# Tail tiles of two attention units searched as one group, and the last keys of a group transposed together

## Chip, cores and metric

The kernel runs on one core of a Trainium2 chip. The metric is the device time of one execution in microseconds; the median of three runs of the kernel before is 1433.77 us (1432.75 to 1434.97). One execution was recorded by the hardware profiler; its span is 1435.2 us. Engines are named as in the profile: PE (TensorE; PEld is its weight load), DVE (VectorE), ACT (ScalarE), POOL (GpSimd), SP (the queue that issues most transfers).

## The reference

A top-k attention is followed by a mixture of experts without dropping. Everything is float32.

```python
# attention: batch 8, heads 8, sequence 576, head width 64
scores = scale * np.matmul(q, k.transpose(0, 1, 3, 2))
kth = np.partition(scores, -32, axis=-1)[..., -32:-31]
scores = np.where(scores >= kth, scores, -1e9)
attn = softmax(scores)                    # exp, sum + 1e-9
attn_out = np.matmul(attn, v)
# experts: 4608 tokens of width 512, 8 experts, hidden width 1024
x = attn_out laid out as (8 * 576, 512)
logits = x @ w_gate
expert_idx = argmax(logits); gate_w = softmax(logits)[expert_idx]
y = relu(x @ w1[expert_idx]) @ w2[expert_idx]   # per token
return gate_w[:, None] * y
```

For each of the 8 x 8 x 576 query rows the 32nd largest of 576 scores has to be found; that is the search which the change regroups.

## The kernel before

**Units and tiles.** Two heads make a unit (128 partitions: two heads of width 64), so there are 4 units a batch and 32 in all. A head has 576 query rows, that is four tiles of 128 rows and a rest of 64. In a unit, tiles 0 to 3 are the first head's full tiles, 4 to 7 the second head's, and tile 8 (the tail) holds the 64 last rows of both heads, in the two halves of the partitions. `groups` (L215) lists what is searched together: four pairs (i, 4+i), and the tail alone, as a group of one tile. That gives 5 groups a unit, 20 a batch, 160 in all (`work`, L721).

**One group.** `products` (L240) multiplies queries with keys on PE into PSUM, in two halves of 288 keys. `scores` (L256) copies them to SBUF on ACT. `fold` and `fold_on` (L263, L273) take, on DVE, the maximum and the minimum of pairs of scores, so that few candidates remain (168 columns a tile). `search` (L296) finds the 32nd largest with MAX8 (L309, L322) and MATCH_REPLACE8 (L329), four rounds. `depths` (ACT, L352), `less` (POOL, L361) and `weights` (ACT exponential, L372) turn the scores into unnormalised weights with zeros for what isn't selected. `transposed` (L377) turns the weights on PE: four transposes of 128 keys a tile (L385) and one of the last 64 keys a tile (L394), each copied out by ACT (L388 or L390 to `wT`, L397 to `wTt`).

**The end of a unit.** `outputs` (L399) multiplies the transposed weights with the values (L413), in two halves of 288 query rows. Each head has its own 64 output rows in PSUM, and for each head there are four products with `wT` (128 keys each) and one with `wTt`, whose upper 64 partitions are zeros. Then the result is transposed back and multiplied with the gate weights (L419 to L424). `divisors` (DVE, L434), `logits` and `rows` (POOL, L443, L453) apply the softmax sums. `ending` (L783) is a generator that puts these steps at named places of the following groups.

**Order.** `loop` (L879) goes over the groups, and the order of the instructions on PE, ACT and DVE is the order in which the code is written. In group i, DVE first folds group i+1 (L896), then searches group i; the second part of the fold (`fold_on`) is put ahead of the last round of that search. PE is three groups ahead with score products (`AHEAD`, L709), and transposes the group before.

**Expert work as filler.** When a batch's rows are routed, they are scattered to buckets, and full blocks of 128 rows are put through an expert on PE. A block is 16 pieces. `pieces` (L752) puts some of them between the attention's operations; a credit that grows with the group's tiles, times a share that depends on the group's place in the unit (L909 to L918), says how many. The first pieces come in the third batch; what can't be ready earlier is done after the attention, on PE with little else.

In the code below, the lines to follow are the tail's special cases (`len(tiles)`), the last-key transposes, and the products with `wTt`.

Of the kernel before, what the change touches and what calls it, by code (L numbers as in the profile page):

```python
# [35 lines left out]
def kernel(  # L36
# [39 lines left out]

    nc = tc.nc
    B, U, P, _, S = qk.shape
    N, Dm = out.shape
    E = moe_w_gate.shape[1]  # L80
# [33 lines left out]
    def open_pools(st, exact):  # L114
        for name, bufs in (
            ("load", 2), ("att", 2), ("wtp", 1), ("xp", 1 if exact else 2), ("small", 2),
            ("wp", 1 if exact else 2), ("mlp", 2),
        ):
            setattr(k, name, st.enter_context(tc.tile_pool(name=name, bufs=bufs)))
        for name, bufs in (("ps_s", 2), ("ps_t", 2), ("ps_m", 2)):  # L120
            pool = tc.tile_pool(name=name, bufs=bufs, space=bass.MemoryType.PSUM)
            setattr(k, name, st.enter_context(pool))
        k.exact = exact
        k.apart = False
        k.unit = 0

    def load_unit(b, u, parts=False):
        n = SimpleNamespace(b=b, u=u)
        qkb = k.load.tile([P, 2, S], F32, name="qkb")
        if parts:  # L130
            nc.scalar.dma_start(qkb[:, 0, 0:P], qk[b, u, :, 0, 0:P])
            nc.sync.dma_start(qkb[:, 1, :], qk[b, u, :, 1, :])
            nc.scalar.dma_start(qkb[:, 0, P:S], qk[b, u, :, 0, P:S])
        else:
            nc.sync.dma_start(qkb, qk[b, u, :, :, :])
        n.q, n.k = qkb[:, 0, :], qkb[:, 1, :]
        return n
# [43 lines left out]
    for n in range(2):  # L181
        t = const.tile([P, KC * P], F32, name=f"oT{n}")
        nc.gpsimd.memset(t[:, S:], 0.0)
# [4 lines left out]
    wTt = const.tile([P, 2, S], F32, name="wTt")  # L188
    nc.gpsimd.memset(wTt[ST:P, :, :], 0.0)
# [25 lines left out]
    groups = [(i, NC + i) for i in range(NC)] + [(2 * NC,)]  # L215
# [13 lines left out]
    def open_unit(n):  # L229
        n.z = k.small.tile([P, NT], F32, name="z")  # L230
        n.over = None if k.exact else doubt[:, n.b * U + n.u, :, :]
# [8 lines left out]
    def products(n, tiles):  # L240
        todo = []
        got = []
        for i in tiles:
            ps = k.ps_s.tile([P, 2, SM], F32, name="sc")
            todo += [(ps, h, rows, cols) for h, rows, cols in parts(i)]
            got.append(ps)
        for half in range(2):
            for ps, h, rows, cols in todo:
                j = half ^ h if len(tiles) == 1 else half
                d = slice(h * D, (h + 1) * D)  # L250
                nc.tensor.matmul(  # L251
                    ps[rows, j, 0:HF], n.q[d, cols], n.k[d, j * HF:(j + 1) * HF], start=True, stop=True
                )
# [9 lines left out]
    def fold(tiles, s):  # L263

        m2 = slice(0, len(tiles))
        f = SimpleNamespace()
        f.h = k.att.tile([P, 2, HF], F32, name="h", bufs=1)
        nc.vector.tensor_tensor(f.h[:, m2, :], s[:, m2, 0, :], s[:, m2, 1, :], op=ALU.max)  # L268
        f.l = k.att.tile([P, 2, HF], F32, name="l")
        nc.vector.tensor_tensor(f.l[:, m2, :], s[:, m2, 0, :], s[:, m2, 1, :], op=ALU.min)  # L270
        return f

    def fold_on(tiles, f):  # L273

        m2 = slice(0, len(tiles))
        f.few = k.att.tile([P, 2, LW], F32, name="few", bufs=3)
        nc.vector.tensor_tensor(f.few[:, m2, 0:QF], f.h[:, m2, 0:QF], f.h[:, m2, QF:HF], op=ALU.max)
        f.hl = k.att.tile([P, 2, QF], F32, name="hl", bufs=1)
        nc.vector.tensor_tensor(f.hl[:, m2, :], f.h[:, m2, 0:QF], f.h[:, m2, QF:HF], op=ALU.min)
# [16 lines left out]
    def search(n, tiles, s, f, then=lambda: None):  # L296

        m_all = range(len(tiles))
        m2 = slice(0, len(tiles))
# [14 lines left out]
        def quiet(r):  # L314

            return r >= (1 if len(tiles) == 2 else 2)

        for r in range(R):
            if r == R - 1:
                then()  # L320
            for m in m_all:
                nc.vector.max(out=tops[:, m, r * 8:(r + 1) * 8], in_=src[m])  # L322
                if quiet(r):
                    tick()
            if r == 0:
                in_turn(nc.gpsimd.tensor_scalar_mul(nbias[:, m2], tops[:, m2, 0], -scale))
            if r < R - 1:
                for m in m_all:
# [4 lines left out]
                    if quiet(r):  # L333
# [4 lines left out]
        nc.scalar.activation(low[:, m2], thr[:, m2], AF.Copy, scale=STEEP)  # L338

        def doubts():  # L340
            c = 2 * tiles[0] if len(tiles) == 2 else 2 * NC
            k.last_pool = in_turn(nc.gpsimd.tensor_tensor(
                n.over[:, c:c + len(tiles), :], f.few[:, m2, QF + 7:LW:8], _inner(thr[:, m2], NL), op=ALU.subtract
# [4 lines left out]
    def depths(tiles, s, low):  # L348

        w = k.att.tile([P, 2, S], F32, name="w", bufs=1 if k.exact else 3)  # L350
        for m in range(len(tiles)):
# [6 lines left out]
    def less(tiles, s, w):  # L358

        for m in range(len(tiles)):  # L360
# [4 lines left out]
    def weights(n, tiles, w, nbias, beside=()):  # L365

        c = 2 * tiles[0] if len(tiles) == 2 else 2 * NC
        for m in range(max(len(tiles), len(beside))):
            for step in beside[m:m + 1]:
                step()  # L370
            if m < len(tiles):
                nc.scalar.activation(  # L372
                    w[:, m, :], w[:, m, :], AF.Exp, scale=scale, bias=nbias[:, m:m + 1],
                    accum_out=n.z[:, c + m:c + m + 1],
                )

    def transposed(n, tiles, w):  # L377

        pair = len(tiles) == 2
        if tiles[0] == 0:  # L380
            n.wT = k.wtp.tile([P, NC, 2, S], F32, name="wT")
        for m, i in enumerate(tiles):
            pm = bank("wTm")
            for c in range(NC):
                nc.tensor.transpose(pm[:, c * P:(c + 1) * P], w[:, m, c * P:(c + 1) * P], ident)  # L385
            pm4 = pm[:, :].rearrange("p (c q) -> p c q", c=NC)
            if pair:
                nc.scalar.copy(n.wT[:, :, m, tiles[0] * P:(tiles[0] + 1) * P], pm4)  # L388
            else:
                nc.scalar.copy(n.wT[:, :, :, SM:S], pm4.rearrange("p c (h q) -> p c h q", h=2))  # L390
        yield
        pt = bank("wTl")
        for m in range(len(tiles)):
            nc.tensor.transpose(pt[0:ST, m * P:(m + 1) * P], w[:, m, SM:S], ident)  # L394
        yield
        q = slice(tiles[0] * P, (tiles[0] + 1) * P) if pair else slice(SM, S)
        nc.scalar.copy(wTt[0:ST, :, q], pt[0:ST, 0:len(tiles) * P].rearrange("p (h q) -> p h q", h=2))  # L397

    def outputs(n, x):  # L399

        oT = oT_of[k.unit % 2]
        k.unit += 1
        for j in range(2):
            q = slice(j * HF, (j + 1) * HF)
            po = bank("po")
            for c in range(KC):
                for h in range(2):
                    r = slice(h * D, (h + 1) * D)
                    if c < NC:
                        lhsT, rhs = n.v[:, c, r], n.wT[:, c, h, q]  # L410
                    else:
                        lhsT, rhs = n.v[:, c, r], wTt[:, h, q]
                    nc.tensor.matmul(po[r, 0:HF], lhsT, rhs, start=(c == 0), stop=(c == KC - 1))  # L413
            yield
            nc.scalar.copy(oT[:, q], po[:, 0:HF])  # L415
            yield
        px = bank("px")
        for t in range(NC):
            nc.tensor.transpose(px[:, t * P:(t + 1) * P], oT[:, t * P:(t + 1) * P], ident)  # L419
        pl = bank("pl")  # L420
        nc.tensor.transpose(pl[:, 0:P], oT[:, SM:], ident)
        lw = 2 * E
        for t in range(KC):
            nc.tensor.matmul(  # L424
                pl[:, P + t * lw:P + (t + 1) * lw], oT[:, t * P:(t + 1) * P],
# [288 lines left out]
    with fast:  # L714
# [6 lines left out]
        work = [(b, u, g) for b in range(B) for u in range(U) for g in groups]  # L721
        per_batch = U * len(groups)
# [60 lines left out]
        def ending(b, u):  # L783
# [11 lines left out]
            yield "relu"  # L795
            next(out_steps)
            yield "small"
            div = divisors(n)
            aside.append(div)
            yield "products"  # L800
# [67 lines left out]

        def turning(i):
            b, u, g = work[i]  # L870
            return transposed(unit[b * U + u], g, w_of.pop(i))

        def multiply(i):
            b, u, g = work[i]
            got_of[i] = products(unit[b * U + u], g)
            if g == groups[-1] and b * U + u + 2 < len(units):
                unit.append(load_unit(*units[b * U + u + 2]))

        def loop():  # L879
# [7 lines left out]
            f_of[0] = fold(work[0][2], s_of[0])  # L887
            fold_on(work[0][2], f_of[0])
            for i, (b, u, g) in enumerate(work):
                n = unit[b * U + u]  # L890
                if g == groups[0]:
                    open_unit(n)

                then = lambda: None
                if i + 1 < len(work):
                    f_of[i + 1] = fold(work[i + 1][2], s_of[i + 1])  # L896
                    then = lambda: fold_on(work[i + 1][2], f_of[i + 1])
                low, nbias, doubts = search(n, g, s_of[i], f_of.pop(i), then)
                at_place("small")
                w_of[i] = depths(g, s_of[i], low)  # L900
                less(g, s_of.pop(i), w_of[i])
# [11 lines left out]
                if b == B - 1 and at >= ARRIVED:  # L913
                    room -= KEEP
                    credit = room * len(g) / sum(len(x[2]) for x in work[i:])
                share = 0.5 if g in (groups[0], groups[-2]) else 1.6 if g == groups[2] else 1.2 if g == groups[1] else 1
# [15 lines left out]
                weights(n, g, w_of[i], nbias)  # L932
# [4 lines left out]
                if g == groups[-2]:  # L937
# [10 lines left out]
            for count, _ in enumerate(late[0][0]):  # L948
                if count == 4:
                    pieces(4)  # L950
            kept = left - ALWAYS * PIECES
            assert kept == KEEP - 4, kept
# [21 lines left out]
    with ExitStack() as outer:  # L974
# [10 lines left out]
        with ExitStack() as st:  # L985
# [7 lines left out]
            with tc.For_i(0, B, 1) as b:  # L993
# [3 lines left out]
                for u in range(U):  # L997
                    n = load_unit(b, u)
                    load_values(n)
                    open_unit(n)  # L1000
                    for g in groups:
                        s, steps = scores(products(n, g))
                        for step in steps:
                            step()
                        low, nbias, _ = search(n, g, s, None)
# [75 lines left out]
```

## Time and profile before

| Engine | busy us | share of the span | instructions |
|---|---|---|---|
| PE | 1288.2 | 90% | 8034 |
| PEld | 874.8 | 61% | 8034 |
| DVE | 1132.7 | 79% | 4717 |
| ACT | 937.0 | 65% | 2097 |
| POOL | 645.4 | 45% | 838 |

| Operation | count in the trace | mean ns |
|---|---|---|
| fold, L268, 128x576 / 128x288 | 128 / 32 | 827 / 437 |
| fold, L277, 128x288 / 128x144 | 128 / 32 | 544 / 877 |
| MAX8 of 168 columns, L322 | 1152 | 321 |
| transpose of 128 keys, L385 | 1152 | 295 |
| transpose of the last 64 keys, L394 | 288 | 297 |
| product with `wT`, L413 | 1024 | 447 |
| product with `wTt`, L413 | 256 | 406 |
| copy to `wTt`, L397, 64x256 / 64x128 | 128 / 32 | 361 / 245 |

A share of busy time is a mean over the span. The attention ends at about 1163 us, and DVE has nearly nothing to do after that, so its 79% of the span is nearly all of the attention's time. A product of float32 leaves two records in the trace, a transpose leaves one. Records of PE overlap, so a mean duration is longer than the step from one start to the next, and it is the step that counts when PE is full. Shapes of L277 show an oddity that matters later: the smaller form has the longer mean.

### The profile page before, as it was taken

The numbers are of one execution on the slowest core, as the hardware profiler recorded it, in microseconds if no ns is written. First come the engines' busy times: TensorE is split into PE (matmuls) and PEld (weight loads), VectorE is DVE, ScalarE is ACT, GpSimd is POOL, SyncE is SP. The second block draws the span as 40 slices with busy tenths as digits, with TensorE's granted clock in tenths as the row PEclk, the third lists the DMA queues.
The fourth block names the chain that finished last, engine by engine and source line by source line (L and its number), as shares of the span: only waits on it lengthen the run. The fifth ranks groups of instructions, "written<-read, shape, count | busy, mean of one in ns | idle before, by whom it ended". The sixth has DMA issues, their size and how long they took to land. (4 is left out here: it accounts for less than half of the span.)

```text
span 1435.2 us, 25500 instructions
## 1 busy us (share of the span) xinstructions
PE 1288.2 (90%) x8034; PEld 874.8 (61%) x8034; DVE 1132.7 (79%) x4717; ACT 937.0 (65%) x2097; POOL 645.4 (45%) x838
## 2 busy tenths in 40 slices
PE   5777787767799989998999999999999999999995
PEld 3444454444566656665766666666667677777673
DVE  7999999999999999999899999999989950000000
ACT  5777777777787778877777778787777751111110
POOL 3445455445555655565454555565446541000000
PEclk8777788897899999999999999999999999999998
DMA  2000011001664166416553464237541749998880
GB/s 76 27 26 26 26 34 52 27 26 47 234 219 151 54 246 217 150 49 244 216 212 112 161 247 158 100 125 283 201 180 51 264 161 327 391 321 318 324 320 22
DMA packets 102224, 230.69 MB, mean 161 GB/s; under 512 B 5182, under 2 KB 25918, under 8 KB 102080
## 3 DMA queue, kind: packets, MB, share of 16 engines
q1 hardware_dynamic: 95328, 208.71, 41.1%
q0 software_dynamic: 6464, 19.97, 3.8%
q8 instruction: 65, 1.06, 0.3%
q14 instruction: 79, 0.65, 0.1%
q10 hardware_dynamic: 288, 0.30, 0.1%
HBM read 207.68 MB, written 22.33 MB: 160 GB/s over the span
## 5 line engine op out<-in xcount | busy, mean ns | idle before, releaser
L361 POOL TENSOR_TENSOR w<-s,w 128x576 f32<-128x576 f32 x288 | 407.6, 1433 | 512.4 <-ACT w L352 512.4
L667 PE MATMUL ph<-xTs,w 128*128 128x128 f32 x2560 | 320.6, 279 | 3.4 <-ACT xTs L644 3.4
L667 PEld LDWEIGHTS ph<-xTs,w 128*128 128x128 f32 x2560 | 302.3, 193 | 34.3 <-issue 29.3
L682 PE MATMUL py<-w,hT 128*128 128x512 f32 x640 | 295.1, 598 | 1.0 <-ACT hT L672 0.7
L322 DVE MAX8 tops<-scr 128x8 f32<-128x168 f32 x864 | 252.5, 321 | 2.3
L251 PE MATMUL sc<-qkb 64*128 64x288 f32 (+1 forms) x1280 | 231.5, 484 | 24.2 <-ACT s L260 19.9
L372 ACT ACTIVATE w<-w,nbias 128x576 f32<-128x576 f32 x288 | 224.6, 789 | 1.5 <-POOL w L361 1.4
L385 PE MATMUL wTm<-ident,w 128*128 128x128 f32 x1152 | 177.7, 295 | 46.5 <-ACT oT L415 25.9
L352 ACT ACTIVATE w<-s,low 128x576 f32<-128x576 f32 x288 | 209.4, 769 | 5.3
L385 PEld LDWEIGHTS wTm<-ident,w 128*128 128x128 f32 x1152 | 138.5, 150 | 100.4 <-ACT oT L415 34.1
L969 DVE CAST any_i<-pd 1x1 int32<-1x1 f32 x1 | 0.1, 147 | 236.7 <-PE pd L967 236.7
L682 PEld LDWEIGHTS py<-w,hT 128*128 128x128 f32 x640 | 113.5, 190 | 111.0 <-issue 107.0
L251 PEld LDWEIGHTS sc<-qkb 64*128 64x128 f32 (+1 forms) x1280 | 120.0, 201 | 99.8 <-issue 41.1
L329 DVE MATCH_REPLACE8 scr<-tops,scr 128x168 f32<-128x168 f32 x576 | 178.6, 314 | 0.0
L260 ACT COPY s<-sc 128x576 f32<-128x576 f32 x288 | 171.3, 644 | 7.2 <-PE sc L251 7.2
L388 ACT COPY wT<-wTm 128x512 f32<-128x512 f32 x256 | 139.5, 601 | 32.4 <-PE wTm L385 32.1
L413 PE MATMUL po<-wT,vb 128*64 128x288 f32 x1024 | 153.6, 447 | 0.6 <-ACT wT L390 0.6
L688 POOL DMA_INDIRECT out_dram<-y,xg x40 | 43.5, 1087 | 212.7 <-ACT y L696 200.5
L268 DVE TENSOR_TENSOR h<-s 128x576 f32<-128x576 f32 (+1 forms) x160 | 119.9, 749 | 18.2 <-ACT s L260 18.2
L309 DVE MAX8 few<-l 128x8 f32<-128x288 f32 x288 | 128.2, 445 | 0.0
L413 PEld LDWEIGHTS po<-wT,vb 128*64 128x64 f32 x1024 | 73.6, 148 | 76.3 <-issue 24.1
L672 ACT ACTIVATE hT<-ph 128x512 f32<-128x512 f32 x80 | 47.8, 598 | 107.1 <-PE ph L667 105.7
(125 smaller groups left out, 1549.6 us busy)
## 6 DMA issues: line engine op xcount, KB each, us to landing
w<-in_moe_w_dram SPq DMA_DIRECT2D x80, 2048.0 KB, 9.2
qkb<-in_qk_dram SPq DMA_DIRECT2D x31, 576.0 KB, 3.8
xg<-x_rows SPq DMA_DIRECT2D x40, 257.0 KB, 9.8
vb<-in_v_dram SPq DMA_DIRECT2D x32, 320.0 KB, 3.1
x_rows<-blank SPq DMA_DIRECT2D x5, 257.0 KB, 10.1
x_rows<-blank POOLq DMA_DIRECT2D x4, 257.0 KB, 8.6
x_rows<-x,posi POOLq DMA_INDIRECT x40, 3.1
out_dram<-y,xg POOLq DMA_INDIRECT x40, 5.9
```

Of the source, the lines that this page charges most:

```text
L251: nc.tensor.matmul(ps[rows, j, 0:HF], n.q[d, cols], n.k[d, j * HF:(j + 1) * HF], start=True, stop=True)
L260: lambda m=m, ps=ps: nc.scalar.copy(s[:, m, :, :], ps[:, :, 0:HF]) for m, ps in enumerate(got)
L322: nc.vector.max(out=tops[:, m, r * 8:(r + 1) * 8], in_=src[m])
L329: nc.vector.match_replace(out=scr[:, m, :], in_to_replace=tops[:, m, r * 8:(r + 1) * 8], in_values=src[m], imm_value=NEG,)
L352: nc.scalar.activation(w[:, m, :], s[:, m, :, :].rearrange("p j k -> p (j k)"), AF.Relu, scale=-STEEP, bias=low[:, m:m + 1],)
L361: k.last_pool = in_turn(nc.gpsimd.tensor_tensor(w[:, m, :], s[:, m, :, :].rearrange("p j k -> p (j k)"), w[:, m, :], op=ALU.subtract)).ins
L372: nc.scalar.activation(w[:, m, :], w[:, m, :], AF.Exp, scale=scale, bias=nbias[:, m:m + 1], accum_out=n.z[:, c + m:c + m + 1],)
L385: nc.tensor.transpose(pm[:, c * P:(c + 1) * P], w[:, m, c * P:(c + 1) * P], ident)
L388: nc.scalar.copy(n.wT[:, :, m, tiles[0] * P:(tiles[0] + 1) * P], pm4)
L413: nc.tensor.matmul(po[r, 0:HF], lhsT, rhs, start=(c == 0), stop=(c == KC - 1))
L667: nc.tensor.matmul(ph[:, f, :], n.w1[:, 0, dt, fc * P:(fc + 1) * P], n.xT[:, dt, :], start=(dt == 0), stop=(dt == DT - 1),)
L682: nc.tensor.matmul(py, hT[:, f, :], n.w2[:, 0, f, :], start=(f == 0), stop=(f == FT - 1))
```

## The change

Two edits go together.

First, the tails of two neighbouring units (u, u+1) form one group of two tiles, placed between the four pairs of u and the four pairs of u+1. There are 9 groups for two units, 18 a batch and 144 in all, and every group has two tiles. The branches for a group of one tile go.

Second, the last 64 keys of a pair's two tiles are transposed together. For this the keys are laid out on the host with the last 64 also in front of them: the first head's tile is multiplied with the keys in their usual order and has its last 64 keys at its end; the second head's tile takes the order that begins with the last 64 keys. The end of one tile's weights and the start of the next are then 128 neighbouring columns, which one transpose turns into 128 partitions: one head's last keys in the upper half, the other's in the lower half. The values get a last block of the same form, with zeros where a head's keys meet the other head's columns, so that one product of full width replaces the two of 64 rows. `wT` and `wTt` become fixed tiles with room for the tails of an even unit behind, and of an odd unit ahead of, the other query rows.

```diff
-    groups = [(i, NC + i) for i in range(NC)] + [(2 * NC,)]
+    def groups(u):
+        first, second = ([((a, i), (a, NC + i)) for i in range(NC)] for a in (u, u + 1))
+        return first + [((u, 2 * NC), (u + 1, 2 * NC))] + second
...
-        nc.vector.tensor_tensor(f.h[:, m2, :], s[:, m2, 0, :], s[:, m2, 1, :], op=ALU.max)
+        nc.vector.tensor_tensor(f.h, s[:, :, 0, :], s[:, :, 1, :], op=ALU.max)
...
         pt = bank("wTl")
-        for m in range(len(tiles)):
-            nc.tensor.transpose(pt[0:ST, m * P:(m + 1) * P], w[:, m, SM:S], ident)
+        if tails(tiles):
+            for a in range(2):
+                nc.tensor.transpose(pt[0:ST, a * P:(a + 1) * P], w[:, 1 - a, SM:S], ident)
+        else:
+            nc.tensor.transpose(pt[:, 0:P], w[:, :, :].rearrange("p m k -> p (m k)")[:, SM:SM + P], ident)
...
-            for c in range(KC):
+            for c in range(NC):
                 for h in range(2):
                     r = slice(h * D, (h + 1) * D)
-                    if c < NC:
-                        lhsT, rhs = n.v[:, c, r], n.wT[:, c, h, q]
-                    else:
-                        lhsT, rhs = n.v[:, c, r], wTt[:, h, q]
-                    nc.tensor.matmul(po[r, 0:HF], lhsT, rhs, start=(c == 0), stop=(c == KC - 1))
+                    nc.tensor.matmul(po[r, 0:HF], n.v[:, c, r], wT[:, c, h, q], start=(c == 0), stop=False)
+            nc.tensor.matmul(po[:, 0:HF], n.v[:, NC, :], wTt[:, q], start=False, stop=True)
...
-        work = [(b, u, g) for b in range(B) for u in range(U) for g in groups]
+        work = [(b, g) for b in range(B) for u in range(0, U, 2) for g in groups(u)]
...
             yield "products"
             next(out_steps)
-            yield "relu"
-            next(out_steps)
+            if u % 2 == 0:
+                yield "relu"
+                next(out_steps)
             yield "small"
             div = divisors(n)
             aside.append(div)
+            if u % 2:
+                yield "relu"
+                next(out_steps)
...
-                    credit = room * len(g) / sum(len(x[2]) for x in work[i:])
-                share = 0.5 if g in (groups[0], groups[-2]) else 1.6 if g == groups[2] else 1.2 if g == groups[1] else 1
+                    credit = room / (len(work) - i)
+                share = {0: 0.5, 1: 1.2, 2: 1.6, 3: 0.5, 2 * NC: 1.4}[tile]
```

An odd unit has no tail group behind it, so in `ending` its late steps come one group earlier. The planner's shares are set anew for the nine groups.

## Prediction

> **What bounds the kernel now.** I read the page's slices first: VectorE (DVE) is at 9 tenths until it stops, TensorE (PE) runs 7 to 8 tenths at a granted clock of 0.7 to 0.8, fills up after a quarter of the span, and alone fills the rest.
>
> ```profile
> PE   5777787767799989998999999999999999999995
> DVE  7999999999999999999899999999989950000000
> PEclk8777788897899999999999999999999999999998
> ```
>
> To put numbers on it I cut the span where a new batch reaches the same place in the loop (start of L268 of every 20th group, from the timeline): two batches without expert work, three with four expert blocks in them (375.19, 517.59, 813.85), two with five (661.54, 960.94), the end of attention, the rest. Columns: stretch, its length, busy time of PE, PEld, DVE, ACT, POOL, then PE clock, DMA.
>
> ```profile
> 98.67:236.67 138.00, 106.14 (x593) 64.16 (x593) 136.59 (x574) 104.76 (x242) 73.17 (x97) 0.79 0.11 36
> 236.67:375.19 138.52, 100.33 (x576) 60.94 (x577) 137.53 (x588) 105.80 (x242) 73.83 (x97) 0.83 0.12 36
> 375.19:517.59 142.40, 134.57 (x904) 92.83 (x904) 141.41 (x589) 113.66 (x257) 77.26 (x100) 0.98 0.47 166
> 517.59:661.54 143.95, 137.19 (x924) 93.85 (x922) 142.96 (x589) 114.36 (x258) 78.96 (x101) 1.00 0.47 166
> 661.54:813.85 152.31, 148.95 (x1002) 104.12 (x1000) 142.78 (x588) 116.98 (x262) 82.42 (x102) 0.99 0.53 188
> 813.85:960.94 147.09, 141.06 (x928) 95.95 (x927) 142.76 (x588) 114.44 (x258) 81.02 (x101) 0.99 0.46 163
> 960.94:1111.69 150.75, 147.38 (x1002) 103.46 (x1000) 142.86 (x589) 117.08 (x262) 82.20 (x102) 1.00 0.52 186
> ```
>
> So there are three regimes. Until 375 us DVE is busy 99% and PE 72 to 77%: DVE sets the time. With four blocks both are near full (DVE 97 to 99%, PE 94.5 to 96%). With five PE is 97.8% full and DVE 94 to 95%: PE sets it. From 1163 us on PE alone works off blocks whose number is fixed. ACT (about 78%) and POOL (56%) have room everywhere.
>
> The timeline shows what DVE's 138 us consist of. Lengths of a group (L268 to next L268) before 375 us have medians 7.02, 7.6, 7.02, 7.12 and 5.34 us for tiles 0, 1, 2, 3 and the lone tail: 34.1 us a unit, 136.4 a batch, and some 1.8 for the routing. The 7.6 holds the three divisor operations (about 0.6). The tail is half of a pair's work but 0.76 of its time, and it brings collisions:
>
> ```profile
> 103.76 1.26 POOL L457 TENSOR_TENSOR x<-x,rz 128x640 f32<-128x640 f32 x1
> 103.88 1.30 DVE L277 TENSOR_TENSOR few<-h 128x144 f32<-128x144 f32 x1
> ...
> 419.95 2.99 POOL L361 TENSOR_TENSOR w<-s,w 128x576 f32<-128x576 f32 x2 [4.05 <-ACT w L352]
> ...
> 420.81 0.87 DVE L277 TENSOR_TENSOR few<-h 128x288 f32<-128x288 f32 x1
> 421.60 1.65 DVE L279 TENSOR_TENSOR hl<-h 128x288 f32<-128x288 f32 x1
> ```
>
> The 128x144 L277 takes 0.29 us when POOL is quiet and ends with POOL's operation when it isn't. The second stall (0.4 and 1.2 us over the usual 0.45) is in a tail's group: being short, it reaches L277 while POOL is still on the pair before it. Such tail groups average 7.08 us after 375 us.
>
> **What the Trainium skill says.** "SBUF — State Buffer", Who interferes with whom: a DVE instruction with two SBUF inputs and a GpSimd instruction that reads SBUF exclude each other for a whole instruction. The trace agrees: 1.30 us against 0.29, ending with POOL. "VectorE: DVE Perf Modes", The TRN2 errata: an fp32 tensor_tensor costs (N+151)/0.96 ns, 457 for 288 elements and 757 for 576; the trace has 447 and 766 at L270, so merging two saves some 0.13 us. "TensorE: Matmul & The Clock Gate", Part 3: matmuls in different column groups of the array run together. The trace agrees: sixteen L413 records (eight matmuls of 64 output rows, two records each) take 2.0 us to the next start, 0.50 a couple, while one full-width L682 matmul of 512 columns takes 0.86, which scaled to 288 columns is 0.48.
>
> **The change, part by part.**
>
> *Tails together, DVE.* 160 groups become 144, all pairs. MAX8 and MATCH_REPLACE8 stay in number, one per tile; 128 fold operations of half size become 64 of full size (0.13 us saved for each two merged), and the lone tail's serial steps go (0.80 us from one MAX8 to the next, where a pair takes 1.07 for two). Nine pairs take 9 x 7.02 = 63.2; the divisors stay, 2 x 0.6. The stall with L457 stays, once a unit, but smaller: the fold now ahead of it is of a pair, 0.6 us longer (0.74+0.74 for 0.44+0.45), so DVE comes 0.7 us into POOL's 1.26 and waits about 0.55 for 1.0. Sum 63.2+1.2+1.1 = 65.5 for two units, against 68.2 now. A batch: 2 x 65.5 + 1.8 = 132.8 against 138.2, **5.4 us less**. Bounds of that wait, 0 and 1.0, make it 3.6 to 7.6.
>
> *Last keys together, PE.* 128 pair groups have one transpose less. In a row of eight a transpose (L385) moves the next start by 0.11 us; by busy time of L394 (63.8 us for 288) it would be 0.22, but that includes the wait for a bank. I take 0.11: 16 a batch, 1.8 us. Outputs: per half two 64-row matmuls with wTt (0.58 us to the next start) become one full one (0.48 by the scaling, at worst the same 0.58). Eight halves a batch x 0.10 = 0.8. Together **2.6 us of PE a batch**; 1.8 to 4.3 by the bounds. The tails' two transposes, their score products and the other products are the same in number.
>
> *ACT.* The wTt copy is 128x128 (L432: 278 ns) in place of 64x256 (361): 1.3 us a batch, hidden behind ACT's idle fifth. The tails' copy is two of 245 ns for two units, as many as now. 16 `low` and 16 `nbias` operations fall away, also hidden.
>
> *DMA.* qk loads grow from 576 to 608 KB, land in 3.8 us by the page and are needed four groups (28 us) later: nothing. The wT tile, one buffer before and after, is written by a unit's first group two groups after the last product that reads it: no new wait. oT and zero fills: set-up only.
>
> *Order.* Each unit's late steps keep their group distance after an even unit and come one group earlier after an odd one (no tail group between). Walking through the planner's loop, expert pieces start at group 49 of 144 (53 of 160 now), 367 of them fall in the loop (368 now), with at most nine in a group, as now; one more is left for the end: +1.0 us (16 us a block of 16 pieces). The last search is of a pair, not a lone tail, so ACT, POOL and ACT have a tile more each (0.8, 1.4, 0.8) before the last transposes, with one piece to cover it: I add 2 us.
>
> **The sum.** Until 375 us, 53 groups or 2.65 batches: 2.65 x 5.4 = **14.3 less**, DVE alone deciding. In batches with four blocks DVE's floor falls to 132.8 and PE's need to 132.0, 134.6 and 138.5. Neither can be hidden behind the other any more; I let PE reach the 97.8% that it reaches with five blocks: 135.0, 137.6, 141.6, which is 7.4+6.3+5.5 = **19.2 less**. With five blocks PE need is 146.3 and 144.8, at 97.8% 149.6 and 148.1: **5.4 less**. The last groups to 1163 us: 1 less. The end: 3 more. Total -14.3-19.2-5.4-1+3 = -36.9: 1433.8 becomes **1397 us**.
>
> **Rivals.**
>
> *PE's use doesn't improve.* Where expert work runs, PE stays at its present 94.5 to 97.8%, because its gaps come from other waits (ACT's evacuation of the transposes' banks, 52 us over the span) and not from DVE. Then those 5.3 batches give only 2.6/0.96 each, 14.4. With -14.3 and +3: 1408. For it: DVE is already 99% busy at PE 94.5%, so PE is not simply pulled by DVE. Against: part of DVE's busy time there is the tail stall, which goes.
>
> *PE nearly full.* With the tail stalls gone PE reaches 99%: four-block batches 133.3, 136.0, 139.9 (24.2 less), five-block ones 147.8, 146.3 (9.0 less); -14.3-24.2-9.0-1+3 gives 1388. For it: windows of 98.8% exist (700 to 800 us). Against: none lasts a whole batch.
>
> *Slower.* The planner's shares for nine groups put 5, 7, 6 and 6 pieces where 7 stood alone, so PE lags in lumps, DVE waits for scores (18 us in all now), and POOL's two tails collide with the folds after them. If every expert batch lost 4 us on its present time, plus the end: 1433.8-14.3+21+3 = 1443. Against: three groups of scores lie ahead, enough for one lump of nine pieces today.
>
> **Chances.** Forecast 0.50, PE unimproved 0.23, PE nearly full 0.21, slower 0.04, and 0.02 for ending where it began. With the bounds of the stall (2.65 x 2 us, either way) and of PE's saving (up to 1.7 us in five batches), the range is 1381 to 1413. Faster 0.94, same 0.02, slower 0.04.
>
> **What will show it.** DVE: the fold's first operation 144 times, always 128x576; group length 7.0 with none of 5.34; a batch before expert work of about 133 us; the fold beside POOL's row scaling still at 0.8 to 1.1 us. PE: 160 last-key transposes for 288, and a full-width output product near 0.48 us. Expert batches: PE share 97 to 98%. I am wrong if the first batches don't shorten by 4 us or more (then tails cost DVE less than their group length says), or if the expert batches keep their PE share and length.

## The result

The changed kernel takes 1400.35 us (median of four runs, 1397.27 to 1401.87) against 1434.37 before: a ratio of 0.9756, 95% interval 0.9728 to 0.9784. That is 34 us less; 1397 was forecast. The execution in the profile is one of the shorter ones, with a span of 1395.5 us.

The slices of the page after look as before, only that DVE has no slice under 9 tenths left in the middle, and PE none from the twelfth slice to the last but one, where two of 8 tenths stood before:

```profile
PE   5777787677899999999999999999999999999995
DVE  7999999999999999999999999999999920000000
PEclk8788878888899999999999999999999999999998
```

The same cuts at each batch (start of L283, the fold's first operation, of every 18th group): stretch, length, busy time of PE, PEld, DVE, ACT, POOL, PE clock, DMA.

```profile
103.96:235.11 131.15, 98.69 (x547) 61.93 (x546) 130.48 (x565) 103.67 (x240) 71.49 (x91) 0.83 0.12 39
235.11:367.27 132.16, 100.26 (x553) 61.58 (x554) 132.00 (x580) 103.76 (x240) 74.62 (x94) 0.84 0.12 39
367.27:502.64 135.37, 131.59 (x870) 92.69 (x871) 135.12 (x580) 111.00 (x253) 77.67 (x97) 0.98 0.50 176
502.64:639.71 137.07, 134.67 (x889) 93.88 (x888) 136.41 (x580) 111.99 (x257) 80.55 (x98) 1.00 0.50 175
639.71:786.79 147.08, 144.63 (x953) 101.43 (x952) 143.93 (x580) 111.89 (x255) 83.09 (x96) 1.00 0.54 195
786.79:928.86 142.07, 140.09 (x910) 98.06 (x909) 141.41 (x580) 114.37 (x262) 81.71 (x101) 0.99 0.49 170
928.86:1075.94 147.08, 144.63 (x953) 101.46 (x952) 143.90 (x581) 111.90 (x255) 83.06 (x96) 1.00 0.53 191
```

| Stretch | before | after | difference |
|---|---|---|---|
| two batches without expert work | 276.5 | 263.3 | -13.2 |
| three batches with four blocks | 433.4 | 414.5 | -18.9 |
| two batches with five blocks | 303.1 | 294.2 | -8.9 |

A batch has 36 tiles in both kernels, and the five batches with expert work hold the same expert products to within 5 of 1744 records, so these stretches compare like with like. Two thirds of what these seven batches gained came where PE was already 94 to 98% busy.

The collision with POOL's row scaling is still there, smaller, as foreseen:

```profile
137.80 1.25 POOL L470 TENSOR_TENSOR x<-x,rz 128x640 f32<-128x640 f32 x1
138.46 0.91 DVE L291 TENSOR_TENSOR few<-h 128x288 f32<-128x288 f32 x1
```

DVE now comes 0.66 us after POOL's start, and loses 0.46 us instead of 1.0.

### The profile page after: what moved, and what is told of

Same layout as the page of the kernel before. It is cut to its first block, busy times and chain, and to the rows that moved or that the text cites. A ratio compares the mean times of both kernels' runs of the same rounds, so it can differ in the third digit from the quotient of the medians.

```text
span 1395.5 us, 24818 instructions
## 1 busy us (share of the span) xinstructions
PE 1267.8 (91%) x7778; PEld 872.2 (62%) x7778; DVE 1106.4 (79%) x4653; ACT 920.6 (66%) x2081; POOL 650.0 (47%) x804
## 5 line engine op out<-in xcount | busy, mean ns | idle before, releaser
L680 PE MATMUL ph<-xTs,w 128*128 128x128 f32 x2560 | 311.7, 278 | 6.0 <-ACT xTs L657 6.0
L269 PE MATMUL sc<-qkb 64*128 64x288 f32 (+1 forms) x1280 | 224.0, 476 | 9.7 <-ACT s L276 5.2
L391 PE MATMUL wTm<-ident,w 128*128 128x128 f32 x1152 | 173.7, 289 | 27.2 <-ACT x L444 17.8
L283 DVE TENSOR_TENSOR h<-s 128x576 f32<-128x576 f32 x144 | 115.9, 805 | 7.9 <-ACT s L276 7.9
```

The costliest lines, as they stand in the source:

```text
L269: nc.tensor.matmul(ps[rows, j, 0:HF], n.q[d, cols], n.k[d, keys], start=True, stop=True)
L391: nc.tensor.transpose(pm[:, c * P:(c + 1) * P], w[:, m, first:first + P], ident)
L680: nc.tensor.matmul(ph[:, f, :], n.w1[:, 0, dt, fc * P:(fc + 1) * P], n.xT[:, dt, :], start=(dt == 0), stop=(dt == DT - 1),)
```

## Experiments

### Which of the two edits brings the gain

Two kernels make one edit each. The first searches tails in pairs and keeps the last keys as they were:

```diff
-            nc.tensor.transpose(pt[:, 0:P], w[:, :, :].rearrange("p m k -> p (m k)")[:, SM:SM + P], ident)
+            for m in range(2):
+                nc.tensor.transpose(pt[0:ST, m * P:(m + 1) * P], w[:, m, SM:S], ident)
...
-            nc.tensor.matmul(po[:, 0:HF], n.v[:, NC, :], wTt[:, q], start=False, stop=True)
+            for h in range(2):
+                r = slice(h * D, (h + 1) * D)
+                nc.tensor.matmul(po[r, 0:HF], n.v[:, NC, r], wTt[:, h, q], start=False, stop=True)
```

> Only the tails of two units are searched together; the last keys of a pair are transposed tile by tile and multiplied in two products of 64 rows, as before (two side effects: keys without the extra block in front, and the table of doubts in bfloat16 to make room). Theory A (DVE sets the time without expert work, PE with it, and the two edits act in different stretches): batches without expert work as short as in the full change, 131 to 132 us; with it PE has some 2.7 us a batch more than in the full change, so 138 to 140 us with four blocks and about 150 with five; in all 1400 + 5 x 2.7 = 1413 us (1408 to 1418). Rival B (all of the gain is DVE's): about 1400. Rival C (all of the gain is PE's): 1425 or more.

The second is the kernel before with the joint transpose, the wide product and their layout of keys and values; `groups` and the planner stay as they were.

```diff
-        for m in range(len(tiles)):
-            nc.tensor.transpose(pt[0:ST, m * P:(m + 1) * P], w[:, m, SM:S], ident)
+        if pair:
+            nc.tensor.transpose(pt[:, 0:P], w[:, :, :].rearrange("p m k -> p (m k)")[:, SM:SM + P], ident)
+        else:
+            nc.tensor.transpose(pt[0:ST, 0:P], w[:, 0, SM:S], ident)
```

> Only the last keys are transposed together and multiplied in one wide product; each tail is still searched alone. Theory A: batches without expert work stay at 138 us, those with it lose at most PE's 2.7 us a batch, total 1434 - 12 = 1422 us (1418 to 1428). Rival B (all of the gain is DVE's): 1434. Rival C (all of it is PE's): about 1405.

Tails alone: 1401.29 us, ratio 0.9768 (0.9753 to 0.9783). Keys alone: 1435.05 us, ratio 1.0007 (0.9996 to 1.0017). By whole runs rival B comes nearest: the tails bring all of the gain, the last keys nothing that could be measured, and theory A, on which the forecast rested, is wrong (it gave 1413 and 1422 us). The stretches tell more. Batches without expert work take 131.2 and 132.1 us with the tails alone, as short as in the full change, and 137.9 and 138.7 with the keys alone. The batches with five blocks, first of the tails alone, then of the keys alone:

```profile
639.42:786.89 147.47, 145.63 (x985) 102.13 (x984) 144.30 (x580) 112.94 (x257) 84.46 (x96) 1.00 0.53 193
929.12:1080.04 150.92, 149.08 (x985) 103.74 (x984) 143.34 (x580) 112.99 (x257) 84.02 (x96) 0.98 0.51 185
```

```profile
660.47:813.51 153.04, 149.37 (x972) 104.49 (x968) 145.11 (x588) 116.32 (x266) 83.17 (x102) 0.98 0.53 188
960.35:1111.71 151.36, 147.69 (x972) 103.39 (x968) 143.90 (x588) 116.45 (x266) 82.32 (x102) 0.99 0.53 186
```

The keys alone leave them at 153.0 and 151.4 us (152.3 and 150.8 before), though PE has fewer records. The tails alone bring the first to 147.5 without taking any product or transpose away. The second, 150.9, is longer because the clock granted to PE fell in it. The same 20 us in the tails alone and in the full change:

```profile
1010.00:1030.00 20.00, 20.00 (x108) 12.90 (x107) 19.16 (x85) 11.70 (x28) 8.48 (x12) 0.83 0.40 152
```

```profile
1010.00:1030.00 20.00, 19.95 (x118) 13.16 (x119) 19.67 (x88) 12.97 (x32) 8.10 (x11) 1.00 0.40 152
```

At 0.83 for 20 us some 3.4 us of PE's work are lost, as much as that batch is longer by (3.8). Seen more closely, a fall is 3.4 us, or twice that, at half the clock. Here are the one of the tails alone and one in the first batch with five blocks of the kernel before:

```profile
1021.40:1028.20 6.80, 6.80 (x13) 3.45 (x13) 5.96 (x29) 1.25 (x4) 2.54 (x4) 0.50 0.66 266
```

```profile
675.50:678.90 3.40, 3.40 (x15) 1.78 (x15) 3.40 (x15) 1.69 (x5) 2.62 (x5) 0.50 1.04 418
```

With half the length of its falls taken off, the two batches with five blocks of one kernel agree:

| Kernel | as measured | length of the falls | falls taken off |
|---|---|---|---|
| before | 152.3, 150.8 | 3.4, none | 150.6, 150.8 |
| keys alone | 153.0, 151.4 | 6.8, 3.4 | 149.6, 149.7 |
| tails alone | 147.5, 150.9 | none, 6.8 | 147.5, 147.5 |
| full change | 147.1, 147.1 | none, none | 147.1, 147.1 |

So in such a batch the tails alone save some 3.2 us (part of that is work on the other side of a cut: 985 records for 1002) and the keys alone 1.0. The saving of the keys doesn't reach the whole run: over the last four batches with expert work the falls of the profiled run are 13.6 us long in all, those before 6.8, and the difference, 3.4 us of time, is as much as the keys save there (3.0). What brings a fall on isn't shown: the one of the kernel before came right after 3.4 us in which PE was busy for only 1.3, that of the tails alone after 3.4 us of small products of the routing, with PE busy throughout. So falls may in part follow from what a kernel does there. Runs of the full change spread over 4.6 us. So differences of 3 us between kernels have to be read from the stretches and their clock, not from one run.

### How much each engine's time counts

The next two leave out most expert products in the attention's stretch (three of four with w1, seven of eight with w2), once from each kernel, so that PE has room everywhere.

```diff
-                for dt in range(DT):
+                last = 0 if clock is not None else DT - 1
+                for dt in range(last + 1):
...
+            if clock is not None:
+                if f == 0:
+                    nc.tensor.matmul(py, hT[:, f, :], n.w2[:, 0, f, :], start=True, stop=True)
...
```

> The changed kernel with most expert products of the attention stretch left out (one of four with w1, one of eight with w2; the rest of the expert work as it is). Theory A: with PE relieved DVE sets the time in every batch, so all of them take 131 to 133 us and PE falls to 80% or less; total about 1350. Rival: expert batches stay above 137 us, because something else that comes with expert work (stores, ACT's copies, POOL's collisions) sets their time; total above 1375.

> The kernel before with the same expert products left out of the attention stretch. Theory A: all batches take 138 to 139 us, total about 1388, some 40 us and more above the changed kernel treated alike: without PE's limit the search of tails in pairs is worth 6 us a batch in the later batches too. Rival: the stalls of the tail groups that come with expert work (7.08 us a group instead of 5.34) stay, and batches take 142 us or more.

They took 1352.73 and 1395.30 us, in one run each. All batches of the changed kernel then last 130.9 to 133.9 us, all of the kernel before 137.1 to 140.1. The third batch of each, changed kernel first:

```profile
366.94:500.51 133.57, 106.20 (x643) 68.39 (x644) 133.41 (x581) 110.60 (x255) 79.03 (x96) 0.89 0.50 178
```

```profile
375.38:514.60 139.22, 110.18 (x677) 71.69 (x676) 138.23 (x589) 112.81 (x257) 77.16 (x100) 0.87 0.47 170
```

PE is at 79 to 80% and DVE at 99%. This is DVE's floor, and the change lowers it by 5.8 us a batch (667.4 against 696.2 us over the five batches). With the whole expert work the same five batches differ by 27.8 us, 5.6 a batch in the mean, but not evenly: 7.0, 6.9 and 5.0 us with four blocks, 3.5 and 3.7 with five, falls taken off. What DVE saves comes through with four blocks, where PE was 94.5 to 96% busy, and only in part with five.

Two more kernels add work to the changed kernel: four transposes a group done twice, and one MAX8 a group done twice.

```diff
-                nc.tensor.transpose(pm[:, c * P:(c + 1) * P], w[:, m, first:first + P], ident)
+                for _ in range(2 if c < 2 else 1):
+                    nc.tensor.transpose(pm[:, c * P:(c + 1) * P], w[:, m, first:first + P], ident)
...
-                    nc.vector.max(out=f.few[:, m, QF + 8 * j:QF + 8 * j + 8], in_=away)
+                    for _ in range(1 if m or j else 2):
+                        nc.vector.max(out=f.few[:, m, QF + 8 * j:QF + 8 * j + 8], in_=away)
```

> The changed kernel with four transposes of each group done twice: by 0.11 us each some 0.44 us more PE work a group, 7.9 us a batch, nothing for DVE. Theory A of the prediction (PE sets the time where there is expert work): 5.3 batches x 7.9 = some 42 us more, total 1440, and nothing without expert work. Theory D (DVE and PE alternate within a batch: only groups with many expert pieces are PE's, and PE can't run ahead of the search): about half or less in expert batches, total 1410 to 1422.

> The changed kernel with one MAX8 of 288 columns in each group done twice: by the trace 0.37 us more DVE work a group, 6.6 us a batch, nothing for PE. Theory A: without expert work batches 6.6 us longer, with it 1 or 2 at most; total 1400 + 18 + 8 = 1426. Theory D (DVE's time counts in all groups that aren't full of expert pieces): 5 us or more in each expert batch as well, total 1445 to 1453.

More PE: 1428.44 us, ratio to the kernel before 0.9955 (0.9940 to 0.9969). More DVE: 1432.93 us, ratio 0.9981 (0.9970 to 0.9993). Both lie between what the two theories gave. What a batch gained in length over the changed kernel:

| Batch | more PE (7.9 us by the step) | more DVE |
|---|---|---|
| without expert work | 0.1, 1.7 | 7.6, 8.3 |
| four blocks | 3.6, 6.5, 2.2 | 6.2, 3.5, 0.6 |
| five blocks | 8.6, 8.5 | 3.3, 1.6 |
| last two of four blocks, falls taken off | 4.7, 3.9 | 3.5, 2.4 |
| five blocks, falls taken off | 6.9, 6.8 | -0.1, -0.1 |

Here the clock decides what is read. With five blocks the changed kernel has no fall, more PE one of 3.4 us in each batch, and more DVE these (batch, then fall):

```profile
670.80:821.15 150.35, 147.26 (x956) 103.11 (x955) 145.06 (x598) 111.20 (x252) 78.97 (x97) 0.98 0.54 191
762.10:768.90 6.80, 6.80 (x13) 3.32 (x13) 6.77 (x37) 1.25 (x3) 2.52 (x4) 0.50 0.70 283
963.86:1112.53 148.67, 145.59 (x956) 102.20 (x955) 146.06 (x598) 111.21 (x252) 79.30 (x97) 0.99 0.53 189
1055.70:1059.10 3.40, 3.40 (x6) 1.35 (x6) 3.40 (x23) 1.25 (x3) 1.97 (x4) 0.51 1.03 425
```

Without expert work only DVE counts; with five blocks added PE work counts for the most part and added DVE work not at all; with four each counts in part, and the two parts make 8.2 and 6.3 us together. As the cuts fall a little differently, the sum of the last three batches is safer: 17.6 of 23.7 us for more PE, 2.2 of some 24 for more DVE. So the three regimes of the prediction are there for *added* work. Group lengths of the changed kernel (start of one fold to the next) suggest how each can count in part: after 367 us the searches of tile 2 in even units and of tile 0 in odd ones have medians of 7.02 us, DVE's own time, while tile 2 in odd units and the tails have 9.2 and 8.6. I read a batch with four blocks as a sum over groups in which now one engine and now the other is last: PE transposes what the search has just found, so it can't work off a heavy group in advance. That reading is from the code and the lengths; no run shows it by itself.

The kernel with more DVE work shows one thing more. Its batches without expert work, 138.8 and 140.5 us, are as long as those of the kernel before (138.0 and 138.5), yet its five batches with expert work take 723.8 us against 736.5. So 12.7 of the 27.8 us remain when DVE's time is put back, though at other places. The last keys can be some 3 of them. What gives the rest isn't shown: the groups of lone tails were longer with expert work (7.08 us for 5.34, by the prediction, which puts it down to POOL), and the planner's shares, too, changed with the pairs of tails. The tails alone have the new shares as well, so no run tells the two apart.

### The planner's shares

```diff
-                share = {0: 0.5, 1: 1.2, 2: 1.6, 3: 0.5, 2 * NC: 1.4}[tile]
+                share = 1
```

> The changed kernel with all shares of the expert planner set to 1 in place of 0.5 to 1.6: the groups that carry a unit's last steps then get as many pieces as the others. If the new shares are part of the gain, PE lags where outputs and pieces meet, DVE waits for scores there, and the total rises by 5 us or more (1405 to 1415). If three groups of scores ahead level it anyway: 1400, within 2 us.

It took 1389.36 us, ratio 0.9678 (0.9647 to 0.9709): 11 us less than the changed kernel, in the direction that neither expectation had. The third and fifth batches, 134.39 and 145.84 us instead of 135.37 and 147.08, and the fourth, 134.39 for 137.07, show it at PE shares of 97.5 to 99.6%:

```profile
366.80:501.19 134.39, 131.02 (x877) 92.76 (x878) 134.23 (x580) 112.16 (x255) 79.59 (x97) 0.98 0.50 177
501.19:635.58 134.39, 133.20 (x889) 93.61 (x890) 134.23 (x581) 112.88 (x257) 79.65 (x98) 1.00 0.51 179
635.58:781.42 145.84, 145.20 (x955) 102.78 (x956) 142.65 (x581) 112.42 (x255) 82.20 (x96) 0.99 0.55 197
```

The five batches take 698.3 us, 10.4 less. So the lumps that the shares make cost 2 us a batch, which fits the view of a sum over groups. This doesn't tell what even shares would do to the kernel before; that wasn't tried.

### The last product of an output half

> The changed kernel with the full-width last product of each output half replaced by its two corners that aren't zero (64 keys by 64 output rows each, at opposite corners of PE's array). The trace has 0.59 us for the wide product to the next start, and 0.10 us more for the product row before it than with two products of 64 rows. If the wide form is what costs, the corners take 0.5 us or less and PE saves some 0.2 us a half, 1.6 us a batch; as PE's savings have shown little effect (last keys alone: none), the total is 1398 to 1400. If any small last product costs as much, PE's steps and the total stay.

```diff
-            nc.tensor.matmul(po[:, 0:HF], n.v[:, NC, :], wTt[:, q], start=False, stop=True)
+            for h in range(2):
+                r = slice(h * D, (h + 1) * D)
+                nc.tensor.matmul(po[r, 0:HF], n.v[r, NC, r], wTt[r, q], start=False, stop=True)
```

1397.33 us, ratio 0.9742 (0.9723 to 0.9761), within the interval of the full change; its five batches take 709.0 us against 708.7. The corners take 0.63 us to the next start, the wide product 0.59, and in both the eight products before them take 2.09. The next keeps all 128 keys, but goes by head, so that all ten products have one form:

```diff
-            nc.tensor.matmul(po[:, 0:HF], n.v[:, NC, :], wTt[:, q], start=False, stop=True)
+            for h in range(2):
+                r = slice(h * D, (h + 1) * D)
+                nc.tensor.matmul(po[r, 0:HF], n.v[:, NC, r], wTt[:, q], start=False, stop=True)
```

> The changed kernel with the last product of an output half made for each head by itself (128 keys, 64 output rows, with the zeros in the values), the form of the eight products before it; the joint transpose stays. The switch of form costs 0.10 us a half in the changed kernel (step of the eight products 2.09 us, 1.99 with the old form, the last product 0.59 either way). If the switch is what eats the saving of the transposes, both steps are 1.99 and 0.59, PE saves 0.8 us a batch, and with 0.8 of PE's time counting in five expert batches the total falls by some 3 us to 1397. If the zeros' side or the joint rhs costs it: no change.

1394.38 us, ratio 0.9711 (0.9684 to 0.9738). Here are the output halves from the timeline of PE (start, duration), of the changed kernel and then of this one:

```profile
664.79 2.16 PE L424 MATMUL po<-wT,vb 128*64 128x288 f32 x16
666.88 0.75 PE L425 MATMUL po<-wTt,vb 128*128 128x288 f32 x2
```

```profile
662.42 2.16 PE L424 MATMUL po<-wT,vb 128*64 128x288 f32 x16
664.41 0.66 PE L427 MATMUL po<-wTt,vb 128*64 128x288 f32 x4
```

The step from the first to the second start is 2.09 us where the form changes and 1.99 where it doesn't, as in the kernel before. The switch is the cost, not the width. The five batches take 705.6 us, 3.0 less, or 4.7 with falls taken off in the last four of them, where some 3 were expected. The median fell by 6, more than that, but the interval touches that of the change, so 3 to 5 us is what the stretches support.

### The collision with POOL

> The changed kernel with POOL's row scaling put one step later, behind the small nbias operation of the next group's search, where DVE is between folds. The collision theory (once a unit the fold waits 0.46 us for POOL, in the changed kernel, and DVE's time is time of the kernel): batches without expert work fall from 131 to 132 us to 129 to 130, those with it by up to 1.8; total 1400 - 8 x 1.8 = 1386 at best, 1388 to 1396 likely. Rival: the stall only moves, since POOL's subtraction for the weights now comes 1.3 us later and meets a fold or delays the exponentials; 1400.

```diff
-    aside = []
+    aside, put_off = [], []
...
+                while put_off:
+                    put_off.pop(0)()
...
-            rows(n, x)
+            if clock is None:
+                rows(n, x)
+            else:
+                put_off.append(lambda: rows(n, x))
```

1402.47 us, ratio 0.9771 (0.9754 to 0.9788): nothing gained, and the two batches without expert work take 132.7 and 134.1 us, longer than 131.2 and 132.2. POOL's nbias operation had stood in line right behind the row scaling anyway; it now goes ahead of it (0.2 us), and the scaling starts 0.50 us before the fold in place of 0.66, so that the fold waits longer (1.08 us at 138.75, for 0.91).

> The changed kernel with POOL's order within a group changed: row scaling directly behind the subtraction for the weights, then the logits, and the doubts last, so that the 1.26 us of row scaling end about when the second fold begins. If the collision costs 0.46 us a unit where DVE sets the time, batches without expert work fall by 1.2 to 1.8 us (to 129.5 to 131) and the total by 4 to 7 us, to 1393 to 1396. Rival: as in the run with the scaling put later, another of POOL's operations meets a fold, and nothing is won: 1400.

```diff
-            logits(n, lg)
             rows(n, x)
+            logits(n, lg)
...
                 less(s_of.pop(i), w_of[i])
-                doubts()
...
                 at_place("rows")
+                doubts()
```

1408.78 us, ratio 0.9818 (0.9791 to 0.9844): 8 us worse. In groups that were aimed at the stall is gone (7.00 us instead of 7.49 and 7.48 in groups 35 and 39). But the batches without expert work take 131.0 and 133.1 us, because other operations now meet POOL. These are lines of the timeline of both engines in the group where the routing table is worked out:

```profile
332.92 1.04 POOL L538 DMA_INDIRECT x_rows<-x,posi  x1
333.37 1.92 DVE L615 TENSOR_SCALAR upto_all<-upto_all 1x9 f32<-1x9 f32 x1
333.98 1.28 POOL L470 TENSOR_TENSOR x<-x,rz 128x640 f32<-128x640 f32 x1
```

An operation on nine numbers starts while POOL's scatter runs and ends with the row scaling right behind it, and the search stands behind it; that group takes 9.22 us instead of 7.46. In the changed kernel the same operation runs inside the same scatter, with no row scaling behind, and isn't held:

```profile
335.04 1.04 POOL L538 DMA_INDIRECT x_rows<-x,posi  x1 [0.16 <-issue]
335.33 0.15 DVE L615 TENSOR_SCALAR upto_all<-upto_all 1x9 f32<-1x9 f32 x1
```

With expert work the batches of four blocks grow by 1.9 to 3.3 us; which operations meet there was not worked out.

> The two before together: products by head, and row scaling first. If both work, their gains add, as one is PE's and the other DVE's: 1390 to 1394. If only one works: that one's time.

1400.32 us, ratio 0.9762 (0.9734 to 0.9790): neither expectation held. By the medians the products by head gain 6.0 us beside the old order and 8.5 beside the new, and the new order loses 8.4 or 5.9; nothing is left of the two. The best of all is the even shares; even shares together with products by head weren't run.

## Why the prediction was right, and where it wasn't

**DVE's work on tails.** Right in size and cause. Nine groups were to take 65.5 us; the medians before 367 us sum to 65.47. The stall of 0.55 us measures 0.46. A batch without expert work fell by 6.9 and 6.4 us instead of 5.4: by the same account it left about 1.8 us for routing, and 0.2 to 1.2 is what remains.

**Where it counts.** The forecast had 14.3 less until 375 us. The marks there (375.19, 367.27) show only 7.9, because group 49 now has 98 tiles behind it, where group 53 had 96; the last groups make up for it. What lies outside the five batches lost 11.9 us in the profiled runs, where the forecast's terms (-14.3, -1, +3) gave 12.3.

**Five batches with expert work.** Forecast 24.6 less, measured 27.8 (26 with falls taken off in the last four of them), so the size was right. The working wasn't: it took PE's need from its busy time, let DVE's relief only raise PE's share to 97.8%, which makes some 11 us, and gave the rest, 2.6 us a batch, to the last keys. The tails alone brought 23.9 us there, 25.6 with falls taken off. PE's idle time (length less busy time) did fall, as foreseen, from 27.3 to 12.4 us, and PE's share in the full change rose to 97.2 to 98.6%. But with the tails alone PE was also busy 9.0 us less in these batches (700.2 for 709.2), and 9.1 us less over the whole span (1279.1 for 1288.2), with the same 8034 records in both and a mean granted clock of 0.94 in both. So part of what the page counts as busy is waiting. Busy time is no need.

**Last keys together.** This is the term that failed. 0.11 us was taken for a transpose, and the mean step did fall by 0.11 (0.28 to 0.17 us in groups of two and of one): 1.7 us a batch. For the outputs the wide product was scaled down from 512 columns to 0.48 us, to save 0.10 a half; it takes 0.59, and the eight products before it 0.10 more, because the form changes between them. So the half costs 0.10 more, 0.8 a batch. The sum is 0.9 us instead of 2.6, and outside the stated bounds of 1.8 to 4.3: the upper bound that I set on the wide product left out what it does to its neighbours. By itself the 0.9 shows in the batches with five blocks (1.0 us each, falls taken off). On top of the tails only 0.4 us each is left of it, and 1.2 us over the last four batches with expert work. Why not more, when added PE work counts for the most part with five blocks, stays open.

**The rivals.** "PE's use doesn't improve" gave these five batches some 14 us and is refuted by the 27.8 and by PE's idle time. "PE nearly full" is what the even shares show (99.6% in the batches with five blocks), not the change. The "slower" rival had a true part: lumps of pieces do cost time, 2 us a batch, though three groups of scores lie ahead; the change gained more than they cost, and the kernel before had uneven shares too.

The two wrong sizes, too much for the keys (some 13 us of the forecast) and too little for the tails, nearly cancelled; that part of the total's being right was luck.

## What to carry to other kernels

When two engines are both above 94% busy, look at the single groups before you say which one bounds a stretch: a stretch can be a sum of groups in which they take turns, and then a saving on either counts, and so does an even spread of filler work. Before a few microseconds between two profiled runs are put down to a change, compare the granted clock in the same stretches. A saved instruction is worth the step to the next start, measured among its real neighbours; a product of another form than those around it can cost what it saves. And moving an operation out of one collision on a shared resource needs a look at everything else that the new place overlaps.

## What the runs showed of the hardware

A change between products of 64 output rows and one of 128, or one of 64 keys by 64 rows, put 0.10 us on the row of products ahead of it, whichever came after. The granted clock fell to half for 3.4 or 6.8 us at a time, and a batch with five blocks, where PE sets the time, was longer by half of that (150.9 for 147.5 us with the tails alone). A VectorE operation with one input and nine elements took 1.92 us, to the end of GpSimd's row scaling, where the scaling stood right behind the scatter in which it began, and 0.15 us where the scatter ran alone. The Trainium skill, "SBUF — State Buffer", Who interferes with whom, counts tensor_scalar among those that can take both ports and so contend; the run agrees for the row scaling. Replacing two dependent chains of MAX8 and MATCH_REPLACE8 on one tile each by one interleaved chain on two tiles cut a round from 2 x 0.80 to 1.07 us.
